# Two loads of keys and queries issued by ScalarE, and two copies moved to VectorE

## The chip, the cores and the metric

The kernel runs on one core of a Trainium2 chip. Times are device microseconds of one execution, from the first to the last work of the core and what lies around it. A core has five engines, each with its own instruction stream in order: TensorE (PE) for matrix products, VectorE (DVE), ScalarE (ACT), GpSimd (POOL) and SyncE (SP), which here only issues transfers between the memory of the chip and the buffers of the core. The engines wait for one another and for transfers by semaphores.

## What is computed

The reference has two parts. The first is gated linear attention over 4 batches, 8 heads, 768 positions and 48 features per head:

```
f = 1 / (1 + exp(-f_logit))
for t in range(S):
    state = f[:, :, t, :, None] * state + k[:, :, t] (outer) v[:, :, t]
    y[:, :, t] = q[:, :, t] @ state
x = y, heads side by side: (4, 768, 384)
```

The second is a gated block with a mixing over positions:

```
h = max(x @ w_in, 0);  u, v = halves of h (512 features each)
v_n = (v - mean(v)) / sqrt(var(v) + 1e-6)
v_s = w_spatial @ v_n (over positions) + b_spatial
out = (u * v_s) @ w_out
```

## The kernel before, in words

The 4 x 768 positions are cut into 24 units of 128 positions, six for each batch. Each unit passes through the attention in chunks, with all eight heads at once, and its result is transposed, split into a high and a low part and used in the products of the second half.

The order of the work isn't found by a planner. It is written out by hand, as a list of words (PLAN, lines 44 to 113), and each word is one step on one unit: `k:0` is step k on unit 0. The program walks through the list and emits each step, so on each engine the instructions stand in the order of the list. A second list (BESIDES, lines 116 to 123) names the steps that are done in the other way that their function knows, for the most part on another engine: `c:2` stands in it, so the clamp of unit 2 is GpSimd's and not VectorE's.

The steps that matter at the start, for unit n:

- **LF** (line 354) loads the logits of the forget gate into the first plane of the input buffer `fkq` (three such buffers, taken in turn by n mod 3, so that unit 3 takes unit 0's). For the first eight units it is a load of 128 x 384 values, 192 KB. **LK** (line 361) loads keys and queries into the second and third plane, 512 KB. **LQ** (line 365) loads values, 192 KB. **LV** (line 297) loads words of a weight, 768 KB. SyncE issues all of them.
- **c** (line 369) clamps the logits, **e** (line 373) takes two activations of them on ScalarE, **z** (line 378) forms running sums on TensorE with a triangular matrix.
- **g** (line 396) and **h** (line 391) take exponentials of the sums on ScalarE. g writes into the first plane of `fkq`.
- **k** (line 401) multiplies the keys by g's result and **q** (line 405) the queries by h's, both on VectorE. k is the last reader of the first plane, so LF of three units later waits for it.
- **X** (line 424) forms the scores of the unit on TensorE, with the queries and, beside them in the same operand, an identity matrix. **m** (line 441) masks them on VectorE, **w** (line 437) copies the part that came from the identity on ScalarE, **YS**, **kv** and **Yq** (lines 477, 449, 486) are further products on TensorE, **r0**, **r1**, **r2** (lines 458, 466, 473) carry the state on.
- **kq** (line 271) puts that identity beside the queries, by two copies from `ident` into buffer i of `q`. It is done once for each of the three buffers, on ScalarE for i = 0, on VectorE for i = 1 (it stands in BESIDES) and on GpSimd for i = 2. **kz** (line 257) clears a part of two accumulators with two memsets on VectorE.

The table of functions of ScalarE is loaded ahead of all this (line 157). In the list the words begin so:

```
LF:0 constants kq:0 LF:2 c:2 kz c:0 e:0 LF:1 c:1 LK:0 e:2 e:1 z:0 g:0 z:2 LK:1 kq:1 k:0 LK:2 h:0 q:0 LQ:0 z:1
D:1,2,512 g:1 k:1 LV:1 X:0 LF:3 ...
```

So SyncE issues LF:0, LF:2, LF:1, LK:0, LK:1, LK:2, LQ:0, LV:1, LF:3 in this order, VectorE does its memsets, c:0, c:1, kq:1, k:0, q:0, k:1, and ScalarE the table, kq:0, e:0, e:2, e:1, g:0, h:0, g:1.

Of the kernel before, what the change touches and what calls it, by code (L numbers as in the profile page):

```python
# [29 lines left out]
P = 128  # L30
# [15 lines left out]
    D:1,2,512 g:1 k:1 LV:1 X:0 LF:3 LQ:1 m:0 h:1 q:1 g:2 k:2 fm:1 LV:0 w:0 YS:0 kv:0 r0:0 X:1 r1:0 c:3 Yq:0 ca:V,1 LF:5
    fm:0 e:3 LK:3 z:3 LF:4 m:1 ct:V,1 r2:0 h:2 w:1 ys:0 YS:1 kv:1 q:2 xt:0 X:2 r0:1 r1:1 c:5 Yq:1 ca:V,0 g:3 xh:0 xl:0
    m:2 k:3 D:2,2,512 r2:1 h:3 q:3 w:2 ys:1 e:5 LQ:2 YS:2 LQ:3 c:4 e:4 ct:V,0 LK:5 X:3 kv:2 w:3 ch:V,0 r0:2 r1:2 m:3
    ch:V,1 xt:1 cl:V,0 z:4 z:5 cl:V,1 xh:1 xl:1 Yq:2 r2:2 YS:3 kv:3 r0:3 fm:2 LF:6 g:4 LK:4 k:4 V:0,0 g:5 h:4 q:4 c:6
    ys:2 xt:2 r1:3 xh:2 xl:2 LU:0 LQ:4 k:5 LK:6 ca:U,0 ct:U,0 e:6 V:0,1 vr:0,1 Yq:3 X:4 w:4 fm:3 ch:U,0 r2:3 h:5 m:4 z:6  # L50
    kq:2 vr:0,0 V:0,2 cl:U,0 ys:3 q:5 YS:4 kv:4 g:6 k:6 r0:4 vr:0,2 nm:0,0 r1:4 X:5 m:5 LF:7 c:7 e:7 z:7 LU:1 ca:U,1
    ct:U,1 xt:3 vc:0,0 fm:5 fm:4 r2:4 h:7 w:5 h:6 q:6 vc:0,2 U:0,0,1 ur:0,0,1 Yq:4 ys:4 LQ:5 YS:5 kv:5 r0:5 LK:7 q:7
    vc:0,1 xh:3 xl:3 g:7 k:7 X:6 LW:2,0 Yq:5 ch:U,1 w:6 xt:4 xh:4 m:6 cl:U,1 LQ:6 xl:4 ys:5 V:0,3 LF:8 c:8 sq:0,0 sq:0,1
    sq:0,2 xt:5 xh:5 X:7 LF:9 na:0,0 r1:5 xl:5 nb:0,0 nc:0,0 w:7 e:8 LQ:7 YS:6 kv:6 r0:6 LF:10 m:7 vh:0,1 vl:0,1 r1:6
    r2:6 z:8 vh:0,0 wh:2,0 vl:0,0 U:0,0,2 V:0,5 YS:7 Yq:6 LW:0,1 c:9 e:9 fm:6 kv:7 U:0,1,3 h:8 q:8 g:8 vr:0,5 U:0,0,3
    ys:6 k:8 X:8 r0:7 r1:7 Yq:7 fm:8 z:9 LQ:9 LW:1,0 LB LQ:8 LF:11 bs:0,5 r2:7 ur:0,0,2 wh:0,1 fm:7 m:8 wl:2,0 wl:0,1
    ur:0,0,3 h:9 q:9 vr:0,3 g:9 k:9 LW:0,0 U:0,1,1 xt:6 vh:0,2 vl:0,2 ur:0,1,3 bs:0,3 w:8 ys:7 V:0,4 vr:0,4 xh:6 wh:1,0
    YS:8 kv:8 r0:8 LQ:10 X:9 w:9 fm:9 LF:12 bs:0,4 r1:8 na:0,1 xl:6 wh:0,0 nb:0,1 wl:1,0 m:9 c:10 e:10 xt:7 xh:7 nc:0,1
    xl:7 r2:8 vn:0,5 vh:0,5 vn:0,4 vh:0,4 V:1,0 Yq:8 YS:9 kv:9 vn:0,3 vh:0,3 vl:0,5 r0:9 wl:0,0 r1:9 vl:0,3 vl:0,4 V:1,1
    vr:1,1 U:0,0,0 S:0,0,2 LO:1 moe ca:O,1 ct:O,1 z:10 vr:1,0 c:11 e:11 sg:0,0,2 r2:9 h:10 g:10 q:10 k:10 ys:8 ch:O,1  # L60
    S:0,0,0 sg:0,0,0 sm:0,0,2 z:11 S:0,0,3 sg:0,0,3 cl:O,1 LQ:11 LW:2,1 wh:2,1 wl:2,1 xt:8 xh:8 xl:8 sh:0,0,2 sl:0,0,2
    X:10 Yq:9 m:10 h:11 q:11 fm:11 bs:1,0 fm:10 g:11 k:11 bs:1,1 ys:9 w:10 c:12 e:12 V:1,2 S:0,0,1 ur:0,0,0 vr:1,2 z:12
    LW:1,1 wh:1,1 wl:1,1 sg:0,0,1 sm:0,0,1 sh:0,0,1 sm:0,0,0 sh:0,0,0 xt:9 xh:9 X:11 YS:10 bs:1,2 sm:0,0,3 w:11 kv:10
    r0:10 m:11 r1:10 r2:10 na:1,0 sl:0,0,0 h:12 g:12 S:0,1,3 sl:0,0,1 q:12 LF:13 LO:0 ca:O,0 k:12 sg:0,1,3 S:0,1,2 Yq:10
    ys:10 ur:0,1,1 xl:9 YS:11 kv:11 X:12 r0:11 Yq:11 c:13 nb:1,0 r1:11 e:13 ct:O,0 ch:O,0 z:13 h:13 g:13 sg:0,1,2
    S:0,1,0 xt:10 fm:13 xh:10 nc:1,0 vn:1,2 vn:1,1 q:13 S:0,1,1 vh:1,1 w:12 LF:15 LQ:12 LF:14 sg:0,1,0 xl:10 sh:0,0,3
    sl:0,0,3 vn:1,0 c:14 vh:1,2 cl:O,0 m:12 vl:1,2 U:0,1,2 ur:0,1,2 V:1,3 ys:11 xt:11 O:0,0,0 sm:0,1,3 vr:1,3 sh:0,1,3
    sl:0,1,3 LQ:13 k:13 YS:12 kv:12 r0:12 X:13 xh:11 xl:11 Yq:12 sg:0,1,1 c:15 V:1,4 U:0,1,0 ys:12 e:15 z:15 e:14 z:14
    bs:1,3 oc:0,0,0 r1:12 r2:12 LF:16 fm:12 m:13 mr1 h:14 q:14 LQ:14 O:0,0,1 ur:0,1,0 sm:0,1,0 oc:0,0,1 w:13 g:14
    O:0,0,2 k:14 c:16 vh:1,0 sm:0,1,1 sh:0,1,1 sh:0,1,0 fm:14 YS:13 kv:13 r0:13 sm:0,1,2 sh:0,1,2 X:14 Yq:13 r1:13  # L70
    vl:1,1 LQ:15 r2:13 sl:0,1,0 vl:1,0 h:15 vr:1,4 V:1,5 sl:0,1,2 vr:1,5 bs:1,5 bs:1,4 na:1,1 sl:0,1,1 nb:1,1 nc:1,1
    vn:1,4 vn:1,5 g:15 U:1,0,1 ur:1,0,1 fm:15 ys:13 oc:0,0,2 od:0,0,1 vn:1,3 U:1,1,3 ur:1,1,3 vh:1,5 m:14 vl:1,5 k:15
    vh:1,3 vl:1,3 vh:1,4 q:15 vl:1,4 LF:17 od:0,0,0 O:0,1,2 O:0,1,0 oc:0,1,2 od:0,1,2 S:1,0,0 sg:1,0,0 YS:14 e:16 w:14
    kv:14 LQ:16 X:15 r0:14 oc:0,1,0 Yq:14 ys:14 r1:14 r2:14 z:16 h:16 q:16 fm:16 w:15 m:15 U:1,0,0 ur:1,0,0 xt:12
    S:1,0,2 S:1,1,3 g:16 k:16 X:16 LF:18 w:16 sm:1,0,0 sg:1,1,3 sm:1,1,3 mr0 c:17 e:17 c:18 YS:15 kv:15 LQ:17 m:16 r0:15
    r1:15 LF:19 z:17 r2:15 h:17 g:17 k:17 sh:1,0,0 O:0,1,1 fm:17 oc:0,1,1 e:18 sl:1,0,0 q:17 S:1,0,1 sg:1,0,1 xt:14
    Yq:15 ys:15 xh:12 xl:12 X:17 LF:20 sg:1,0,2 YS:16 kv:16 r0:16 r1:16 sm:1,0,1 r2:16 S:1,0,3 S:1,1,0 c:19 c:20 Yq:16
    z:18 h:18 fm:18 w:17 q:18 m:17 YS:17 kv:17 g:18 k:18 ys:16 X:18 sg:1,0,3 od:0,0,2 LQ:18 sg:1,1,0 LF:21 r0:17 Yq:17
    xt:13 xh:14 xl:14 od:0,1,0 e:19 z:19 h:19 g:19 U:1,0,3 ur:1,0,3 e:20 V:2,2 vr:2,2 ys:17 w:18 xh:13 U:1,0,2 ur:1,0,2
    V:2,0 vr:2,0 sm:1,0,3 m:18 k:19 q:19 X:19 LF:22 c:21 r1:17 YS:18 kv:18 LQ:20 LQ:19 z:20 sm:1,0,2 xl:13 m:19 sh:1,0,3  # L80
    sh:1,0,1 xt:15 xh:15 w:19 bs:2,0 sh:1,0,2 sl:1,0,2 xl:15 e:21 r0:18 r1:18 sl:1,0,1 r2:18 xt:17 S:1,1,1 xh:17 xl:17
    fm:19 h:20 g:20 k:20 xt:16 xh:16 V:2,1 q:20 Yq:18 ys:18 YS:19 kv:19 r0:19 sg:1,1,1 r1:19 r2:19 z:21 X:20 w:20
    S:1,1,2 LF:23 m:20 h:21 vr:2,1 sl:1,0,3 O:1,0,0 bs:2,1 fm:21 g:21 sh:1,1,3 Yq:19 ys:19 YS:20 kv:20 LQ:22 k:21
    sg:1,1,2 q:21 X:21 bs:2,2 na:2,0 nb:2,0 r0:20 sl:1,1,3 xl:16 nc:2,0 vn:2,0 vn:2,1 c:22 e:22 z:22 V:2,4 O:1,0,2 c:23
    e:23 w:21 r1:20 r2:20 m:21 fm:20 oc:1,0,0 h:22 q:22 oc:1,0,2 vh:2,1 od:0,1,1 LQ:21 U:1,1,2 xt:18 g:22 k:22 Yq:20
    YS:21 kv:21 r0:21 ys:20 X:22 w:22 r1:21 z:23 r2:21 vn:2,2 ur:1,1,2 vr:2,4 h:23 g:23 fm:23 q:23 m:22 U:1,1,0 k:23
    U:1,1,1 xh:18 Yq:21 vh:2,2 ur:1,1,1 ys:21 YS:22 kv:22 r0:22 r1:22 sm:1,1,1 X:23 m:23 ur:1,1,0 fm:22 flag sm:1,1,0
    xt:19 O:1,0,1 sh:1,1,1 sl:1,1,1 w:23 xt:20 xh:19 xl:19 oc:1,0,1 vh:2,0 r2:22 LQ:23 YS:23 od:1,0,0 kv:23 r0:23 Yq:22
    ys:22 sh:1,1,0 check Yq:23 xl:18 bs:2,4 U:2,0,1 ys:23 mst LY:1 V:2,5 V:2,3 sm:1,1,2 sh:1,1,2 LY:2 xh:20 LY:3 ts:1
    ts:3 vl:2,0 sl:1,1,0 vl:2,1 vr:2,5 bs:2,5 sl:1,1,2 V:3,0 U:2,0,0 vr:2,3 bs:2,3 na:2,1 nb:2,1 nc:2,1 vn:2,3 O:1,1,2  # L90
    U:2,0,3 U:2,0,2 O:1,1,1 th:1 ur:2,0,1 vn:2,5 vh:2,5 vl:2,2 ts:2 LY:4 ts:4 od:1,0,2 vn:2,4 xl:20 V:3,2 th:4 vl:2,5
    tl:4 vh:2,4 vl:2,4 tl:1 ur:2,0,3 th:2 vh:2,3 vl:2,3 xs:2,1,1 P:2,0,2 th:3 tl:3 ur:2,0,0 oc:1,1,1 oc:1,1,2 od:1,1,2
    xs:2,1,3 xs:2,1,2 xt:23 xh:23 xl:23 tl:2 mwin ah:2,1,1 P:2,0,1 P:2,1,2 P:2,1,1 p1:2,0 xs:2,0,1 xs:2,0,3 xs:2,0,2
    ah:2,0,2 ur:2,0,2 p1:2,1 xs:2,0,4 ah:2,0,3 V:3,1 xt:22 c1:2,0 ah:2,1,2 al:2,1,2 al:2,0,2 xt:21 P:2,0,6 xs:2,1,4
    ah:2,1,4 P:2,1,6 c1:2,1 al:2,0,3 p2:2,0 V:3,5 P:2,0,7 xh:22 xl:22 xh:21 ah:2,1,3 al:2,1,3 vr:3,2 bs:3,2 vr:3,0
    sm:2,0,1 sh:2,0,1 al:2,1,4 al:2,1,1 p2:2,1 V:3,4 sl:2,0,1 ah:2,0,1 al:2,0,1 sm:2,0,0 P:2,1,5 p3:2,0 xl:21 bs:3,0
    vr:3,1 bs:3,1 na:3,0 nb:3,0 ah:2,0,4 al:2,0,4 load vr:3,4 vr:3,5 V:3,3 vr:3,3 bs:3,3 U:2,1,0 bs:3,5 P:2,0,5 p5:2,0
    bs:3,4 nc:3,0 na:3,1 nb:3,1 nc:3,1 P:2,0,4 P:2,1,7 c4:2,0 sm:2,0,2 vn:3,0 vh:3,0 O:1,1,0 oc:1,1,0 vn:3,1 vn:3,4
    P:2,1,4 P:2,0,3 p5:2,1 U:2,1,2 vn:3,5 od:1,1,0 vh:3,4 vn:3,2 vh:3,1 sh:2,0,0 vl:3,0 vn:3,3 c5:2,1 p3:2,1 vl:3,4
# [905 lines left out]
```

## Time and profile before

| | |
|---|---|
| time, median of 3 runs | 340.78 us (339.2 to 341.7) |
| the profiled execution | 337.91 us, its span 336.2 us |
| granted TensorE clock | 0.999 of full speed |
| TensorE busy | 324.4 us, 96% of the span |
| VectorE busy | 252.4 us, 75% |
| ScalarE busy | 182.7 us, 54% |
| GpSimd busy | 39.7 us, 12% |
| transfers | 38.37 MB, 114 GB/s over the span |

The span runs from the first to the last instruction of the profiled execution; its own time is 1.71 us longer. A share of busy time is a mean over stages that have different limits, so the rows below are read by stage. In a timeline a row is one instruction or several of one kind merged (x3), and the bracket at its end says how long the engine stood idle before it, and what ended that. In the chain of waits each piece is what the next one waited for. Issue of a transfer and its landing are two things: the queue of SyncE is busy only with the issue.

### The profile page before, as it was taken

How to read it: one execution, taken by the hardware profiler on the slowest of the kernel's cores; microseconds unless marked ns; L12 is line 12 of the kernel's file. 1: busy time of each engine (PE TensorE's matmuls, PEld its weight loads, DVE VectorE, ACT ScalarE, POOL GpSimd, SP SyncE). 2: the span in 40 equal slices, each digit the busy share in tenths (PEclk: the TensorE clock that was granted, in tenths of full speed). 3: DMA queues.
4: the chain of work that ended last, by engine and by line, in shares of the span. 5: the costliest groups of instructions: out<-in, count | busy, mean ns of one | idle time of the engine just before them, and what ended most of it. 6: DMA issues, size and time to landing. Idle time of an engine off the chain costs nothing.

```text
span 336.2 us, 10500 instructions
## 1 busy us (share of the span) xinstructions
PE 324.4 (96%) x4558; PEld 303.5 (90%) x4558; DVE 252.4 (75%) x498; ACT 182.7 (54%) x389; POOL 39.7 (12%) x44
## 2 busy tenths in 40 slices
...
GB/s 230 368 225 280 268 176 225 218 173 47 152 89 237 41 89 155 82 62 126 137 120 142 96 73 202 156 0 24 2 0 0 49 0 25 71 0 26 48 34 118
DMA packets 16581, 38.37 MB, mean 114 GB/s; under 512 B 1552, under 2 KB 11792, under 8 KB 16528
## 3 DMA queue, kind: packets, MB, share of 16 engines
...
q8 instruction: 38, 0.62, 0.7%
...
HBM read 32.90 MB, written 4.72 MB: 112 GB/s over the span
## 4 chain that ended last, share of the span: by engine, by line
PE 93%; DMA 3%; DVE 1%; ACT 1%; issue 1%; SPq 0%; DVEq 0%; ACTq 0%
PE mm L664 15%; PE mm L547 13%; PE mm L650 13%; PE mm L803 12%; PE mn L739 8%; PE bp L432 5%; PE mm L739 5%; PE bp L496 4%; PE bp L484 3%; PE mn L803 3%; PE mn L650 3%; PE mm L509 2%; PE bp L456 2%; PE mn L547 2%; DMA fkq<-fkq 2%; DMA fkq<-fn 1%
## 5 line engine op out<-in xcount | busy, mean ns | idle before, releaser
L371 POOL TENSOR_SCALAR fkq<-fkq 112x512 f32<-112x512 f32 (+1 forms) x13 | 22.5, 1729 | 140.2 <-DMA fkq<-fkq 121.8
L789 DVE TENSOR_TENSOR gl<-uT,gh 128x384 fp32r<-128x384 f32 x29 | 16.6, 580 | 19.9 <-ACT gh L785 19.6
L785 ACT CAST gh<-uT 128x384 fp32r<-128x384 f32 x29 | 14.4, 511 | 20.0 <-DVE uT L781 9.8
L392 ACT ACTIVATE F<-fkq 112x512 f32<-112x512 f32 x16 | 10.1, 632 | 26.6 <-DVE fkq L381 14.9
L432 PE MATMUL bp<-q,fkq 48*64 48x112 f32 x768 | 23.6, 260 | 0.1
L403 DVE SCALAR_TENSOR_TENSOR fkq<-fkq 112x512 f32<-112x512 f32 x24 | 16.7, 694 | 5.9 <-ACT fkq L397 4.7
L432 PEld LDWEIGHTS bp<-q,fkq 48*64 48x64 f32 x768 | 19.0, 133 | 2.1 <-issue 1.4
L664 PE MATMUL mm<-w_sph,vnh 128*128 128x384 f32 x96 | 20.1, 345 | 0.0
L381 DVE TENSOR_TENSOR_SCAN fkq<-runs,fkq 112x512 f32<-112x512 bf16 x16 | 19.4, 1217 | 0.5 <-ACT fkq L376 0.4
L664 PE MATMUL mm<-w_spl,vnh 128*128 128x384 f32 x96 | 19.5, 338 | 0.0
L664 PE MATMUL mm<-w_sph,vnl 128*128 128x384 f32 x96 | 19.5, 338 | 0.0
L547 PE MATMUL mm<-w_inh,xTh 128*128 128x512 f32 x63 | 19.2, 412 | 0.0
L650 PE MATMUL mm<-xTh,w_inh 128*128 128x384 f32 x78 | 18.7, 348 | 0.0
L442 DVE TENSOR_TENSOR sc<-bp,mask 128x512 f32<-128x512 f32 x24 | 16.4, 684 | 2.5 <-ACT W L438 2.1
L407 DVE TENSOR_TENSOR q<-fkq,F 112x512 f32<-112x512 f32 x24 | 16.7, 694 | 2.1 <-ACT F L392 2.0
L547 PE MATMUL mm<-w_inl,xTh 128*128 128x512 f32 x63 | 18.1, 396 | 0.0
L547 PE MATMUL mm<-w_inh,xTl 128*128 128x512 f32 x63 | 18.0, 394 | 0.0
L650 PE MATMUL mm<-xTl,w_inh 128*128 128x384 f32 x78 | 17.9, 338 | 0.0
L650 PE MATMUL mm<-xTh,w_inl 128*128 128x384 f32 x78 | 17.9, 337 | 0.0
L484 PEld LDWEIGHTS bp<-val,sc 64*64 64x64 f32 x768 | 13.9, 134 | 4.3 <-issue 1.5
L484 PE MATMUL bp<-val,sc 64*64 64x48 f32 x768 | 16.1, 220 | 1.4 <-DVE sc L442 0.9
L664 PEld LDWEIGHTS mm<-w_spl,vnh 128*128 128x128 f32 x96 | 17.1, 188 | 0.0
...
## 6 DMA issues: line engine op xcount, KB each, us to landing
...
val<-vv SPq DMA_DIRECT2D x24, 192.0 KB, 4.5
out<-osb SPq DMA_DIRECT2D x24, 192.0 KB, 2.4
fkq<-fkq SPq DMA_DIRECT2D x8, 512.0 KB, 5.5
...
fkq<-fn SPq DMA_DIRECT2D x8, 192.0 KB, 4.1
...
```

The lines of the kernel that those rows point to most:

```text
L371: (nc.gpsimd if beside("c", n) else nc.vector).tensor_scalar(f, f, -LOGIT_MOST, None, op0=ALU.max)
L381: return nc.vector.tensor_tensor_scan(f[0:DP], runs, f[0:DP], 0.0, op0=ALU.mult, op1=ALU.add)
L403: nc.vector.scalar_tensor_tensor(k, f, 1.0 / F_LEAST, k, op0=ALU.min, op1=ALU.mult)
L407: nc.vector.tensor_tensor(q_of(n)[:, :, :, 0:C], *(x.rearrange("p (j c t) -> p j c t", c=T // C, t=C) for x in (parts(n)[2], Fs[n % 2])), ...
L432: nc.tensor.matmul(sc[to, e, cs], k[dr, at:at + C], q_of(n)[dr, j, chunk], start=True, stop=True)
L484: nc.tensor.matmul(y[to, e, cs], s[rows, keys[e]], v[rows, hd], start=j == 0, stop=False, skip_group_check=True)
L547: nc.tensor.matmul(acc, xs[:, c, ut * P:(ut + 1) * P], ws[:, c, G:FF], start=i == 0, stop=i == 3 * KX - 1)
L650: nc.tensor.matmul(acc[:, 0:TH], ws[:, kx, cs], xs[:, kx, :], start=i == 0, stop=i == 3 * KX - 1)
L664: nc.tensor.matmul(acc[:, 0:TH], vns.of((b, ks))[va][:, cs], w_sp_s[wb][:, ks, th * TH:(th + 1) * TH], start=i == 0, stop=i == 3 * KS - 1,)
L739: nc.tensor.matmul(mm.of(user)[:, 0:TH], x, y, start=n == ks == 0 and i not in (3, 6, 7), stop=n == ks == 2, skip_group_check=True,)
L789: nc.vector.tensor_tensor(lo, uTs.of((b, th, c)), hi.bitcast(F32), op=ALU.subtract)
L803: nc.tensor.matmul(acc[:, ms], gs.of((b, th, c))[ga][:, ts], w_out_s[wb][:, c, ms], start=c == cs[0] == 0 and ga == wb == 0, stop=c == cs[ ...
```

## The change

LK:0 and LK:2 are issued by ScalarE, and they stand right behind the constants in the list, ahead of LF:2 and LF:1. kq:0 is done by VectorE and stands behind kz, ahead of c:0. Everything else stands in the same order as before. LK:1, and LK of all other units, stay with SyncE. SyncE's order becomes LF:0, LF:2, LF:1, LK:1, LQ:0, LV:1, LF:3.

```diff
 PLAN = """
-    LF:0 constants kq:0 LF:2 c:2 kz c:0 e:0 LF:1 c:1 LK:0 e:2 e:1 z:0 g:0 z:2 LK:1 kq:1 k:0 LK:2 h:0 q:0 LQ:0 z:1
+    LF:0 constants LK:0 LK:2 LF:2 c:2 kz kq:0 c:0 e:0 LF:1 c:1 e:2 e:1 z:0 g:0 z:2 LK:1 kq:1 k:0 h:0 q:0 LQ:0 z:1 D:1,2,512
...
 BESIDES = """
...
-    sm:3,0,1 P:3,1,5 sm:3,0,2 U:3,1,3 P:3,1,3
+    sm:3,0,1 P:3,1,5 sm:3,0,2 U:3,1,3 P:3,1,3 kq:0 LK:0 LK:2
...
     def step_LK(n):
         b, u = divmod(n, NU)
-        nc.sync.dma_start(ins[n % 3][:, 1:3], fkq[b, u, :, 1:3])
+        (nc.scalar if beside("LK", n) else nc.sync).dma_start(ins[n % 3][:, 1:3], fkq[b, u, :, 1:3])
```

The other lines of PLAN hold the same words, broken into lines elsewhere.

## Rows read from the trace of the kernel before

**Rows 1.** The page's chain that ended last, its share of the span by engine.

```profile
PE 93%; DMA 3%; DVE 1%; ACT 1%; issue 1%; SPq 0%; DVEq 0%; ACTq 0%
```

**Rows 2.** Windows: length, busy us of each engine (instructions), granted clock, DMA share, GB/s.

```profile
40.00:240.00 200.00, 200.00 (x3233) 185.87 (x3232) 166.53 (x324) 120.58 (x259) 19.51 (x11) 1.00 0.38 122
```

**Rows 3.** Chain of waits in order of time, to 21 us: start, us, what.

```profile
2.19 5.89 DMA fkq<-fkq
...
8.19 0.70 DVE fkq L403
...
8.91 4.73 DMA fkq<-fn
...
13.66 0.62 DVE fkq L371
...
20.55 0.68 PE bp L484 x32
```

**Rows 4.** Timeline of ScalarE, to 8 us: start, us, engine, line, operation, idle before.

```profile
0.80 1.28 ACT L157 ACT_TABLE_LOAD   x1 [0.80 <-PEq L998]
2.10 1.03 ACT L276 COPY q<-ident 48x384 f32<-48x384 f32 x2
3.77 0.52 ACT L375 ACTIVATE fkq<-fkq 128x384 f32<-128x384 f32 x1 [0.65 <-DVE fkq L371]
...
6.40 0.52 ACT L375 ACTIVATE fkq<-fkq 128x384 f32<-128x384 f32 x1
...
7.38 0.58 ACT L397 ACTIVATE fkq<-mm 112x512 f32<-112x512 f32 x1
```

**Rows 5.** Windows of the start, columns as in rows 2.

```profile
1.40:1.80 0.40, 0.00 (x0) 0.00 (x0) 0.25 (x4) 0.40 (x1) 0.33 (x2) 1.00 0.00 0
1.80:3.40 1.60, 0.00 (x0) 0.00 (x0) 0.65 (x3) 1.31 (x3) 0.50 (x3) 1.00 0.90 269
3.40:4.20 0.80, 0.00 (x0) 0.00 (x0) 0.34 (x1) 0.42 (x1) 0.22 (x1) 1.00 0.67 109
...
5.00:16.00 11.00, 8.72 (x204) 7.57 (x206) 7.81 (x15) 7.63 (x15) 1.02 (x4) 1.00 1.02 366
```

**Rows 6.** Timeline of VectorE and GpSimd, 1 to 14 us.

```profile
1.68 0.79 DVE L259 MEMSET bp<- 32x384 f32 x2
...
3.38 0.36 DVE L371 TENSOR_SCALAR fkq<-fkq 128x384 f32<-128x384 f32 x1 [0.92 <-DMA fkq<-fn]
3.98 1.17 POOL L371 TENSOR_SCALAR fkq<-fkq 128x384 f32<-128x384 f32 x1 [1.63 <-DMA fkq<-fn]
6.00 0.36 DVE L371 TENSOR_SCALAR fkq<-fkq 128x384 f32<-128x384 f32 x1 [2.26 <-DMA fkq<-fn]
6.28 0.72 DVE L276 COPY q<-ident 48x384 f32<-48x384 f32 x2
...
9.96 0.69 DVE L403 SCALAR_TENSOR_TENSOR fkq<-fkq 112x512 f32<-112x512 f32 x1 [0.47 <-ACT fkq L397]
...
10.80 0.69 DVE L442 TENSOR_TENSOR sc<-bp,mask 128x512 f32<-128x512 f32 x1 [0.15 <-PE bp L432]
...
13.66 0.61 DVE L371 TENSOR_SCALAR fkq<-fkq 128x384 f32<-128x384 f32 x1 [0.21 <-DMA fkq<-fn]
```

**Rows 7.** Timeline of SyncE's queue, 0 to 4 us.

```profile
0.81 1.34 SPq L357 DMA_DIRECT2D fkq<-fn  x3
2.19 1.38 SPq L363 DMA_DIRECT2D fkq<-fkq  x3
```

**Rows 8.** DMA issues near 0.81, 1.72, 2.65, 3.14: KB each, us to landing.

```profile
fkq<-fn SPq DMA_DIRECT2D x1, 192.0 KB, 2.6
...
fkq<-fn SPq DMA_DIRECT2D x1, 192.0 KB, 4.3
...
fkq<-fkq SPq DMA_DIRECT2D x1, 512.0 KB, 6.7
...
fkq<-fkq SPq DMA_DIRECT2D x1, 512.0 KB, 7.5
```

More of the change, by code (lines that the diff above doesn't have):

```diff
@@ L44 @@
 PLAN = """
-    LF:0 constants kq:0 LF:2 c:2 kz c:0 e:0 LF:1 c:1 LK:0 e:2 e:1 z:0 g:0 z:2 LK:1 kq:1 k:0 LK:2 h:0 q:0 LQ:0 z:1
[L46 to L99, printed above, removed]
@@ L100 @@
-    c4:2,1 c3:2,0 c5:2,0 sm:2,0,3 vh:3,5 vl:3,5 vh:3,3 U:2,1,1 vl:3,3 xs:3,0,1 sl:2,0,0 ur:2,1,2 sm:2,1,2 U:3,0,0
-    P:2,1,3 ur:3,0,0 P:3,1,2 c3:2,1 U:2,1,3 ah:3,0,1 sh:2,0,2 vh:3,2 sh:2,0,3 od:1,0,1 xs:3,1,1 xs:3,1,3 vl:3,2 vl:3,1
-    P:3,1,1 sl:2,0,2 sl:2,0,3 O:2,0,0 O:2,0,1 oc:2,0,1 ur:2,1,1 sm:2,1,1 r1:23 sh:2,1,1 sl:2,1,1 U:3,0,3 oc:2,0,0
-    od:2,0,0 od:1,1,1 ah:3,1,3 ur:2,1,0 ur:2,1,3 sm:2,1,3 O:2,0,2 oc:2,0,2 od:2,0,2 P:3,0,1 U:3,0,1 P:3,1,4 xs:3,1,2
-    p1:3,0 xs:3,0,3 xs:3,0,2 p1:3,1 od:2,0,1 al:3,1,3 sm:2,1,0 sh:2,1,0 P:3,0,2 c1:3,1 xs:3,1,4 ah:3,1,2 al:3,1,2
@@ L105 @@
-    P:3,1,6 p2:3,1 U:3,0,2 al:3,0,1 P:3,0,5 xs:3,0,4 sl:2,1,0 ah:3,0,3 ur:3,0,1 al:3,0,3 c1:3,0 sm:3,0,0 U:3,1,0 P:3,1,7
-    ah:3,0,2 al:3,0,2 P:3,0,6 p3:3,1 c4:3,1 sh:2,1,2 sl:2,1,2 ah:3,1,1 al:3,1,1 U:3,1,1 ah:3,1,4 p2:3,0 sh:2,1,3
-    sl:2,1,3 P:3,0,7 P:3,0,4 p5:3,0 sm:3,0,1 sh:3,0,1 sl:3,0,1 ur:3,0,2 ur:3,0,3 p3:3,0 c5:3,0 sm:3,0,3 sh:3,0,3
-    ah:3,0,4 P:3,1,5 O:2,1,0 oc:2,1,0 od:2,1,0 O:2,1,2 oc:2,1,2 od:2,1,2 U:3,1,2 ur:3,1,2 p5:3,1 O:2,1,1 oc:2,1,1
-    od:2,1,1 sh:3,0,0 al:3,0,4 c4:3,0 sm:3,0,2 sh:3,0,2 sl:3,0,3 sm:3,1,2 sh:3,1,2 ur:3,1,0 sl:3,0,2 c5:3,1 sl:3,1,2
@@ L110 @@
-    sl:3,0,0 al:3,1,4 U:3,1,3 ur:3,1,3 sm:3,1,3 ur:3,1,1 sh:3,1,3 P:3,0,3 c3:3,0 sm:3,1,0 O:3,0,2 P:3,1,3 O:3,0,1
-    O:3,0,0 sh:3,1,0 sl:3,1,3 c3:3,1 sm:3,1,1 sh:3,1,1 sl:3,1,1 oc:3,0,0 od:3,0,0 oc:3,0,1 od:3,0,1 oc:3,0,2 od:3,0,2
-    sl:3,1,0 O:3,1,2 oc:3,1,2 O:3,1,0 oc:3,1,0 O:3,1,1 oc:3,1,1 end od:3,1,2 od:3,1,0 od:3,1,1
+    LF:0 constants LK:0 LK:2 LF:2 c:2 kz kq:0 c:0 e:0 LF:1 c:1 e:2 e:1 z:0 g:0 z:2 LK:1 kq:1 k:0 h:0 q:0 LQ:0 z:1 D:1,2,512
+    g:1 k:1 LV:1 X:0 LF:3 LQ:1 m:0 h:1 q:1 g:2 k:2 fm:1 LV:0 w:0 YS:0 kv:0 r0:0 X:1 r1:0 c:3 Yq:0 ca:V,1 LF:5 fm:0 e:3 LK:3
```

63 lines of the change are left out of this document (added).

## The prediction

> **What bounds the kernel now.** I read the chain of waits first. TensorE holds 93% of it [rows 1], and the windows say where: from 40 to 240 us it is busy for all of the 200 us [rows 2], and the chain enters TensorE at 20.55 us and hardly leaves it again [rows 3]. From there on the end follows TensorE's start one for one: what the change is worth is by how much that entry moves. Everything that is edited stands in the first five microseconds, so I read the chain in order of time up to there. It comes out of a load of SyncE that is issued at 2.19 and lands 5.89 us later, at 8.08 [rows 3]. That is LK:0, the keys and queries of unit 0. VectorE's k:0 waits for it and starts at 8.19; it frees the first plane of the buffer, so SyncE issues LF:3 at 8.91, which lands at 13.63 and lets VectorE start c:3 at 13.66. VectorE then works almost without a stop until TensorE takes the chain over.
>
> Two more views give the room beside this chain. ScalarE's timeline [rows 4]: e:0, e:2, e:1, g:0 in this order. g:0 starts at 7.38 straight behind e:1, and ends at 7.96. So k:0, which needs g:0 and LK:0, waits only about 0.2 us for the load (8.19 against 7.96 plus the 0.03 or so that an issue takes). The DMA windows [rows 5]: 269 GB/s up to 3.4 us, 109 from 3.4 to 4.2, and 366 from 5 to 16 us with the share of busy time at 1.02. The transfer engines are full from 5 us on, and have a hole of about 0.8 us before.
>
> **The change, part by part.** All terms are against the profiled execution, 337.91 us, of which 336.2 are the span and 1.71 lie around it. It stands 2.87 under the median of 340.78, so I carry differences over, not times.
>
> *The copies of kq:0.* On ScalarE two copies (1.03 together, from 2.10) go away [rows 4]; on VectorE two of the same shape come, 0.72 together as the pair of kq:1 shows [rows 6]. They stand behind the two memsets of kz, which end at 2.47, and ahead of c:0, which starts at 3.38 when LF:0 lands: 2.47 + 0.72 = 3.19 fits, with 0.19 to spare. Cost nothing; without that cover (LF:0 landing earlier) at most 0.72 less the wait that is left. No consumer is near: X:0 reads them, and it stands behind k:0 and q:0, after 8.19.
>
> *The two issues on ScalarE.* Three issues on SyncE take 1.38 [rows 7], 0.46 each with the gap. On ScalarE no issue is shown. If each costs the same, LK:0 and LK:2 take 0.92. Behind the table load, which ends at 2.08 [rows 4], that is over at 3.00, ahead of e:0 at 3.77: nothing. For the lower bound nothing is gained, as e:0 waits for c:0 anyway; for the upper one, issues of three times this length would push e:0 by 1.1. I take zero: an issue costs about that much in every row of rows 7.
>
> *What SyncE no longer issues.* Its order becomes LF:0, LF:2, LF:1, LK:1, LQ:0, LV:1. LK:1 is issued at 2.19 instead of 2.65, LQ:0 near 2.65 instead of 3.61, LV:1 about 0.95 earlier. k:1 waits for g:1, not for LK:1 (2.65 + 6.7 = 9.35 [rows 8], k:1 starts at 9.96 [rows 6]), so the earlier LK:1 is worth nothing by itself. LK:2 lands at 3.14 + 7.5 = 10.64 [rows 8], and its first reader on VectorE stands behind m:0 and q:1, both later (m:0 starts at 10.80 [rows 6]): nothing to gain there either.
>
> *When LK:0 lands.* The trace has no transfer on a second queue, so this is bounded. Early end: it is there before g:0 ends. Then k:0 starts at 7.99 instead of 8.19, 0.20 gained; q:0, X:0 and m:0 follow, but m:0 can't start ahead of k:1's end (9.96 + 0.69 = 10.65, against 10.80), so 0.15 is left; and LF:3, issued 0.2 earlier into engines that have used their hole, can take away what is left of VectorE's wait before c:3, 0.21 [rows 6]. The sum is 0.36 at most. Late end: LK:0 shares the engines with LK:1 and lands only when LK:1 does now, at 9.35: k:0 1.2 later, of which the wait before c:3 gives 0.21 back, so +1.0. Now it lands at 8.08 behind three small loads, alone in front. I take 8.1 again: about 0.1 us earlier at the issue (2.08 against 2.19) and bytes in the hole (0.8 us at 366 less 109 GB/s are 0.2 MB, 0.55 us of later traffic) on one side, LK:1's bytes between its own on the other. Term: 0.
>
> *What the loads of forget logits lose.* LF:0, LF:2 and LF:1 are ahead of e:0, e:2, e:1, and these ahead of g:0. LF:1 is issued at 1.72 and lands 4.3 later, near 6.0 [rows 8]; c:1 starts at 6.00 and e:1 at 6.40 [rows 4, 6], when e:2 (two activations of 0.52 behind c:2, which ends at 3.98 + 1.17 = 5.15) has ended near 6.3. There is no slack left: each microsecond that LF:1 is later is one at g:0. With LK:0 issued behind the table load its first bytes come, as LF:0's did (issued at 0.81, first bytes after 1.8 us [rows 5]), about 1 us later, near 3.1, when LF:0 has nearly landed; what can be hit is the rest of LF:1. Bounds 0 and +1.6 (next part); I take 0, because in the stretch where LF:1 finishes the engines carry the least [rows 5].
>
> Sum: 0. Forecast: **no change that can be measured, 340.8 us**. Its own range is -0.4 to +0.4.
>
> A rule of the Trainium skill speaks against any gain: DMA: Bandwidth & Descriptors, section "Issuing engines are not separate DMA queues", says that loads issued by ScalarE and SyncE run on the same 16 engines and interleave, so that a second issuer saves only issue time. By it the late end above is the likely one and the sum would be that of the second rival; no run here shows two queues at once yet.
>
> **The rivals.** *First, slower: the forget logits come late.* If ScalarE's sequencer sends LK:0 while the table load still runs, it is issued at about 0.8, level with LF:0, and LK:2 right behind. Then each of the three small loads (197 KB) carries as many bytes of the large ones with it. LF:0 comes 197 KB late, 0.7 at 269 GB/s; LF:2 393 KB late, 1.46, so at 5.4 instead of 3.95, just ahead of c:2's start at 3.98; c:2 on GpSimd takes 1.17 [rows 6], e:2 ends near 7.7; LF:1 590 KB late, 1.6 at 366 GB/s, lands near 7.55, c:1 and e:1 follow and g:0 starts near 8.93 instead of 7.38. k:0 then starts at 9.55, +1.36; LF:3's load of 4.7 us had about 2.2 of queue in it (LF:0 took 2.6 [rows 8]), so it is in time, and the wait before c:3 gives 0.21 back: +1.1, 341.9. It decides as soon as c:1 starts later than 6.1. For it: no slack before g:0. Against: the copies of kq:0 started 0.02 behind the table load's end, as if ScalarE took things in turn, but a DMA issue isn't such an operation. Chance 0.2.
>
> *Second, slower: LK:0 shares with LK:1.* Issue behind the table load, but the engines serve both queues evenly, and LK:0 lands between 8.1 and 9.35; the hole's 0.55 speaks for less than the late end. Taking 9.0, k:0 is 0.9 late: +0.7, 341.5. Chance 0.2.
>
> *Third, faster: the hole is filled.* LK:0 lands before 7.96 and LF:3 in time: -0.35, 340.4. For it: 109 GB/s where 366 are possible. Against: VectorE gets only the two short waits of the early end. Chance 0.2.
>
> The forecast has 0.35; the 0.05 left are for things that I can't price, such as an issue on ScalarE that is several times as long, or a fixed cost of a second queue outside the span.
>
> **How the numbers follow.** All cases lie between -0.4 and +1.1 us. The three runs of the kernel before spread from 1.6 under their median to 0.9 over it, and this enters the range: 340.8 - 0.4 - 1.6 = 338.8, 340.8 + 1.1 + 0.9 = 342.8; I end it at 342.6, since both upper ends together are less likely. About 1%, 3.4 us, is what a measurement of this kernel can tell from no change. A gain of 3.4 is nine times the largest that the waits allow: 0.04, for what the spread or something unseen may do. A loss of 3.4 is three times the largest price: 0.05. Within 1%: 0.91.
>
> **What will show it.** In the changed profile: issues of LK:0 and LK:2 on ScalarE's queue, with their start against the table load's end at 2.08 (first rival or not); c:0 still at 3.4 with kq:0's copies in front of it; c:1 at 6.0 and g:0 at 7.4 (LFs not late); k:0's start against g:0's end (LK:0's landing); GB/s between 3.4 and 4.2 us (hole filled or not); c:3's wait; and TensorE's entry into its unbroken run at 20.55 give or take 0.4, with the same work behind it. The prediction is wrong if that entry moves by more than 1.5 us, or if it doesn't and the span changes all the same.

## The result, and the profile after

The changed kernel takes 341.78 us (median of 20 runs, 339.88 to 343.45), the kernel before 340.14 (20 runs, 337.91 to 341.70). The ratio is 1.0064, with a 95% interval from 1.0048 to 1.0080: about 2.2 us slower (1.6 to 2.7); the two medians alone lie 1.6 apart. Ratios leave out executions more than 1.5% above the fastest of their kernel, in which the granted clock was 0.985 of full speed or less. The result is inside the range and within 1%, but it isn't the likeliest case of the prediction: it is the first rival's mechanism, at twice its price.

From the page of the profile after, its span, TensorE's busy time, and the second queue (packets, MB, share of 16 engines):

```profile
span 339.8 us, 10500 instructions
...
PE 326.3 (96%) x4558; PEld 304.3 (90%) x4558; DVE 253.0 (74%) x500; ACT 181.5 (53%) x387; POOL 40.9 (12%) x44
...
q10 hardware_dynamic: 288, 1.05, 0.8%
```

It is 10500 instructions and 38.37 MB, as before; 1.05 MB of these now pass through a second queue, q10. The timeline of the start answers to [rows 4, 6, 7]:

```profile
0.80 1.28 ACT L154 ACT_TABLE_LOAD   x1 [0.80 <-PEq L995]
...
0.83 0.88 ACTq L360 DMA_DIRECT2D fkq<-fkq  x2
...
2.19 0.83 SPq L360 DMA_DIRECT2D fkq<-fkq  x1
2.38 0.71 DVE L273 COPY q<-ident 48x384 f32<-48x384 f32 x2
...
4.71 0.36 DVE L368 TENSOR_SCALAR fkq<-fkq 128x384 f32<-128x384 f32 x1 [1.62 <-DMA fkq<-fn]
...
6.33 1.95 PE L383 MATMUL mm<-tri,fkq 128*64 128x128 f32 x16 [6.33 <-ACT fkq L373]
6.63 1.17 POOL L368 TENSOR_SCALAR fkq<-fkq 128x384 f32<-128x384 f32 x1 [3.82 <-DMA fkq<-fn]
7.52 0.49 DVE L368 TENSOR_SCALAR fkq<-fkq 128x384 f32<-128x384 f32 x1 [2.45 <-DMA fkq<-fn]
7.84 0.52 ACT L372 ACTIVATE fkq<-fkq 128x384 f32<-128x384 f32 x1 [1.65 <-POOL fkq L368]
...
9.79 0.58 ACT L394 ACTIVATE fkq<-mm 112x512 f32<-112x512 f32 x1
...
10.40 0.69 DVE L400 SCALAR_TENSOR_TENSOR fkq<-fkq 112x512 f32<-112x512 f32 x1 [1.75 <-ACT fkq L394]
...
12.76 0.60 ACT L394 ACTIVATE fkq<-mm 112x512 f32<-112x512 f32 x1 [1.91 <-PE mm L383]
```

Line by line: ScalarE's queue issues the two loads at 0.83, while the table load of 0.80 to 2.08 still runs. VectorE's copies of kq:0 fit in front of c:0, as expected. But c:0 starts at 4.71 instead of 3.38, c:2 on GpSimd at 6.63 instead of 3.98, c:1 at 7.52 instead of 6.00, e:2 at 7.84, and g:0 at 9.79 instead of 7.38. k:0 no longer waits for its load (its bracket names ScalarE) and starts at 10.40 instead of 8.19 all the same.

The issues near 0.83, 0.81, 1.3, 1.25 and 1.72 (KB each, us to landing), which answer to [rows 8]:

```profile
fkq<-fkq ACTq DMA_DIRECT2D x1, 512.0 KB, 4.3
fkq<-fn SPq DMA_DIRECT2D x1, 192.0 KB, 3.9
...
fkq<-fkq ACTq DMA_DIRECT2D x1, 512.0 KB, 6.0
fkq<-fn SPq DMA_DIRECT2D x1, 192.0 KB, 5.2
...
fkq<-fn SPq DMA_DIRECT2D x1, 192.0 KB, 5.8
```

The logits land 3.9, 5.2 and 5.8 us after their issue, at 4.7, 6.5 and 7.5; before it was 2.6 and 4.3 for the first and the last. LK:0 lands at 5.1, ahead of LF:2 and LF:1, where nobody wants it yet. The windows (columns as in rows 2) show that the hole of [rows 5] is filled, 371 GB/s where 109 were:

```profile
1.80:3.40 1.60, 0.00 (x0) 0.00 (x0) 1.25 (x4) 0.29 (x1) 0.96 (x3) 1.00 0.89 225
3.40:4.20 0.80, 0.00 (x0) 0.00 (x0) 0.00 (x0) 0.00 (x0) 0.00 (x0) 1.00 0.94 371
4.20:5.00 0.80, 0.00 (x0) 0.00 (x0) 0.29 (x1) 0.00 (x0) 0.00 (x0) 1.00 1.07 399
```

The chain of waits (start, us, what) now comes out of LF:2, passes through GpSimd's clamp and e:2 and reaches TensorE's sums of units 2 and 1, behind which g:1, k:1 and X:0 stand. It no longer passes through k:0 and LF:3, the path that the prediction had read [rows 3]:

```profile
1.25 5.21 DMA fkq<-fn
...
6.63 1.18 POOL fkq L368
...
8.96 3.68 PE mm L383 x31
```

TensorE's entry into its unbroken run is at 24.08 instead of 20.55 [rows 3]. That is 3.5 us, where the prediction had set 1.5 as the sign that it is wrong. The work behind it has the same length (339.8 - 24.08 = 315.7, before 336.2 - 20.55 = 315.7):

```profile
24.08 0.68 PE L481 MATMUL bp<-val,sc 64*64 64x48 f32 x32 [0.51 <-ACT W L435]
```

This pair of profiles gives 3.5 us, more than the ratio. The first profile of the kernel before is its shortest execution of the 20 (337.91); a second profile of this kernel stands below.

### The profile page after: what moved, and what is told of

Read it like the earlier page. It is cut to its first block, busy times and chain, and to the rows that moved or that the text cites. A ratio compares the mean times of both kernels' runs of the same rounds, so it can differ in the third digit from the quotient of the medians.

```text
span 339.8 us, 10500 instructions
## 1 busy us (share of the span) xinstructions
PE 326.3 (96%) x4558; PEld 304.3 (90%) x4558; DVE 253.0 (74%) x500; ACT 181.5 (53%) x387; POOL 40.9 (12%) x44
## 2 busy tenths in 40 slices
DMA packets 16581, 38.37 MB, mean 113 GB/s; under 512 B 1552, under 2 KB 11792, under 8 KB 16528
## 3 DMA queue, kind: packets, MB, share of 16 engines
q10 hardware_dynamic: 288, 1.05, 0.8%
## 4 chain that ended last, share of the span: by engine, by line
PE 93%; DVE 2%; DMA 2%; ACT 1%; issue 1%; POOL 0%; SPq 0%; DVEq 0%; ACTq 0%; POOLq 0%
PE mm L661 15%; PE mm L544 13%; PE mm L647 12%; PE mm L800 12%; PE mn L736 8%; PE bp L429 6%; PE mm L736 5%; PE bp L493 3%; PE bp L481 3%; PE mn L800 3%; PE mn L647 3%; PE mm L506 2%; PE bp L453 2%; PE mm L383 2%; PE mn L544 2%; DMA fkq<-fn 2%
## 5 line engine op out<-in xcount | busy, mean ns | idle before, releaser
L383 PE MATMUL mm<-tri,fkq 128*64 128x128 f32 (+1 forms) x128 | 10.8, 332 | 7.8 <-ACT fkq L373 7.8
L372 ACT ACTIVATE fkq<-fkq 112x512 f32<-112x512 f32 (+1 forms) x24 | 14.3, 594 | 6.0 <-DVE fkq L368 4.2
```

What stands on the lines that cost most here:

```text
L383: nc.tensor.matmul(z[lo:hi, j * T:(j + 1) * T], f[:, at:at + hi - lo], tri, start=True, stop=True)
```

## The experiments

Starts in us in the profile of each run; the entry is the first product of unit 2's YS on TensorE. Ratios are to runs of the kernel before on the same chip, from 12 runs of each variant (one_queue 6, warm_after 7). In the profiles marked * the granted clock fell to 0.50 of full speed, the 1.2 GHz level, for some us at the start (warm_after from 23 to 29 us, unit1_first from 20 to 26, unit1_first_z2_late from 17 to 20), so their entries and spans don't compare with the others.

| kernel | c:0 | c:2 | c:1 | g:0 | entry | span | ratio (95%) |
|---|---|---|---|---|---|---|---|
| before | 3.38 | 3.98 | 6.00 | 7.38 | 20.55 | 336.2 | |
| before_again | 3.13 | 3.80 | 5.52 | 6.95 | 20.90 | 337.1 | |
| changed | 4.71 | 6.63 | 7.52 | 9.79 | 24.08 | 339.8 | 1.0064 (1.0048 to 1.0080) |
| kq_alone | 3.17 | 3.82 | 5.27 | 6.97 | 20.86 | 336.9 | 1.0014 (0.9988 to 1.0040) |
| loads_alone | 4.57 | 6.42 | 7.24 | 9.57 | 22.46 | 338.2 | 1.0084 (1.0054 to 1.0114) |
| loads_behind_kq | 3.14 | 3.90 | 7.96 | 9.34 | 21.63 | 339.1 | 1.0051 (1.0028 to 1.0074) |
| one_queue | 3.26 | 7.75 | 8.12 | 11.09 | 24.90 | 341.1 | 1.0168 (1.0141 to 1.0195) |
| half_early | 4.29 | 5.45 | 6.48 | 8.61 | 22.21 | 338.4 | 1.0046 (1.0019 to 1.0073) |
| logits_two_queues | 3.74 | 4.08 | 4.46 | 7.42 | 21.51 | 338.7 | 1.0016 (0.9993 to 1.0040) |
| warm_after * | 4.71 | 6.51 | 7.39 | 9.67 | 23.77 | 345.4 | 1.0096 (1.0060 to 1.0132) |
| warm_after_again | 4.76 | 6.56 | 7.42 | 9.71 | 22.16 | 341.2 | |
| warm_before | 3.16 | 3.86 | 5.43 | 7.01 | 21.91 | 338.3 | 1.0039 (1.0008 to 1.0071) |
| unit1_first * | 3.28 | 5.82 | 3.90 | 7.20 | 23.77 | 340.0 | 0.9989 (0.9964 to 1.0013) |
| unit1_first_z2_late * | 3.17 | 5.06 | 3.91 | 7.07 | 21.89 | 337.7 | 1.0044 (1.0014 to 1.0074) |

**The two parts of the change, one at a time.** First the copies alone, with LK:0 and LK:2 where they were:

```diff
-    LF:0 constants kq:0 LF:2 c:2 kz c:0 ...
+    LF:0 constants LF:2 c:2 kz kq:0 c:0 ...      (kq:0 in BESIDES)
```

> Only kq:0 moves to VectorE; all loads as before. Theory (the loss is the two large loads in front of LF:2 and LF:1): no loss; c:0 starts at 3.4, g:0 at 7.4, TensorE's entry at about 20.6, ratio 1.000 (0.998 to 1.002). Rival (the copies on VectorE cost, since in the changed kernel GpSimd's mask copy beside them took 0.70 and not 0.24): c:0 later than 3.6 and a ratio from 1.003 to 1.006.

Measured: 1.0014, the interval holds 1; c:0 at 3.17 and g:0 at 6.97. GpSimd's mask copy took 0.70 here too, and nobody waits for it. Then the loads alone:

```diff
-    LF:0 constants kq:0 LF:2 ...
+    LF:0 constants LK:0 LK:2 kq:0 LF:2 ...       (LK:0, LK:2 in BESIDES)
```

> Only LK:0 and LK:2 move to ScalarE, in front of kq:0, which stays with ScalarE. Theory (early large loads): as the whole change: issues at 0.83, c:0 at 4.7, LF:2 landing near 6.5, g:0 near 9.8, ratio 1.005 to 1.008. Rival (the copies): c:0 at 3.4 and a ratio below 1.003.

Timeline of this kernel:

```profile
4.57 0.36 DVE L368 TENSOR_SCALAR fkq<-fkq 128x384 f32<-128x384 f32 x1 [2.10 <-DMA fkq<-fn]
...
6.42 1.17 POOL L368 TENSOR_SCALAR fkq<-fkq 128x384 f32<-128x384 f32 x1 [4.08 <-DMA fkq<-fn]
...
8.75 2.92 PE L383 MATMUL mm<-tri,fkq 128*64 128x128 f32 x32 [0.62 <-ACT fkq L373]
...
9.57 0.58 ACT L394 ACTIVATE fkq<-mm 112x512 f32<-112x512 f32 x1
```

1.0084, and the same late starts as in the changed kernel. The loss is the loads': the copies alone have 1 in their interval.

**When they are issued.**

```diff
-    LF:0 constants kq:0 LF:2 ...
+    LF:0 constants kq:0 LK:0 LK:2 LF:2 ...       (LK:0, LK:2 in BESIDES)
```

> kq:0 stays with ScalarE and stands in front of LK:0 and LK:2, so that these two are issued by ScalarE only once the identity matrix is there, near 2.1, as the forecast had assumed. Theory (it is the moment of issue that costs): c:0 at 3.4, LF:2 landed by 4.5, g:0 by 8.0, k:0 between 8.0 and 9.0, ratio 0.999 to 1.003. Rival (a second queue takes its share whenever it is issued): LF:1 lands after 7 all the same, g:0 after 8.5, ratio above 1.004.

Timeline of this kernel:

```profile
1.92 0.38 ACTq L360 DMA_DIRECT2D fkq<-fkq  x1
...
3.90 1.17 POOL L368 TENSOR_SCALAR fkq<-fkq 128x384 f32<-128x384 f32 x1 [1.55 <-DMA fkq<-fn]
...
7.96 0.36 DVE L368 TENSOR_SCALAR fkq<-fkq 128x384 f32<-128x384 f32 x1 [4.46 <-DMA fkq<-fn]
...
9.34 0.58 ACT L394 ACTIVATE fkq<-mm 112x512 f32<-112x512 f32 x1
```

The theory, that the moment of issue decides, fell, and the rival held: with the issue at 1.92, LF:0 and LF:2 are in time (c:0 3.14, c:2 3.90), but LF:1, issued at 1.72 and so 0.2 ahead, lands only for c:1 at 7.96. Since g:0 stands behind e:1, it starts at 9.34, nearly as late as in the changed kernel. It isn't the early moment that costs: a large load on the second queue delays the last of the logits also when it is issued behind them. The transfers up to the landing of LF:1 (queue, packets, MB, share) tell how much. First the kernel before, from 1.80 to 5.98 us:

```profile
q1 hardware_dynamic: 552, 1.06, 90.0%
```

Then this kernel, from 1.80 to 7.92:

```profile
q1 hardware_dynamic: 553, 1.03, 53.1%
q10 hardware_dynamic: 212, 0.80, 39.5%
```

SyncE's queue q1 moved as much as before, so it isn't what SyncE now issues earlier that delays LF:1. The 0.80 MB of q10 come on top, about 2 us at the 390 GB/s that the window of 7 to 8 us shows (an estimate), and LF:1 lands 2.0 later.

**Which queue.** The list of the changed kernel, but SyncE issues all of it, so LK:0 and LK:2 stand between LF:0 and LF:2 in one queue.

```diff
-    sm:3,0,1 ... P:3,1,3 kq:0 LK:0 LK:2
+    sm:3,0,1 ... P:3,1,3 kq:0
```

> The list in the order of the changed kernel and kq:0 on VectorE, but LK:0 and LK:2 issued by SyncE: LF:0, LK:0, LK:2, LF:2, LF:1, LK:1 in one queue. Theory (1 MB in front of LF:2 and LF:1, whichever queue it is in): c:0 at 3.4 since LF:0 is alone in front, LF:2 lands near 7, LF:1 near 7.5, g:0 between 9 and 10, ratio 1.004 to 1.008. Rival (the loss comes from two queues taking turns): LF:2 and LF:1 no later than 6, g:0 by 8, ratio below 1.003.

Timeline of this kernel:

```profile
3.26 0.36 DVE L368 TENSOR_SCALAR fkq<-fkq 128x384 f32<-128x384 f32 x1 [0.17 <-DMA fkq<-fn]
...
7.75 1.36 POOL L368 TENSOR_SCALAR fkq<-fkq 128x384 f32<-128x384 f32 x1 [4.93 <-DMA fkq<-fn]
8.12 0.36 DVE L368 TENSOR_SCALAR fkq<-fkq 128x384 f32<-128x384 f32 x1 [4.50 <-DMA fkq<-fn]
...
11.09 0.58 ACT L394 ACTIVATE fkq<-mm 112x512 f32<-112x512 f32 x1
```

The theory's cause held, its size didn't: without any second queue the loss is largest, 1.0168 where at most 1.008 was expected. LF:0 is untouched, LF:2 lands behind all of the 1 MB, g:0 starts at 11.09 (9 to 10 expected). Taking turns isn't the cost; it even softens it. The counterpart takes the second queue for a load of logits and leaves the keys and queries behind them:

```diff
-    LF:0 constants kq:0 LF:2 c:2 ...
+    LF:0 LF:2 constants kq:0 c:2 ...             (LF:2 in BESIDES, step_LF as step_LK in the change)
```

> The kernel before, in which ScalarE issues LF:2 (the 192 KB of logits of unit 2) while SyncE issues LF:0; all keys and queries stay behind the logits on SyncE. Theory (what counts is which bytes are in front of the logits, not the second queue): LF:0 at most 0.5 us later, LF:1 lands 0.4 us earlier or as before, g:0 between 7.0 and 7.6, ratio 0.997 to 1.001. Rival (a second queue itself costs): c:0 after 4.2, g:0 after 8.2, ratio above 1.003.

Timeline of this kernel:

```profile
3.74 0.36 DVE L371 TENSOR_SCALAR fkq<-fkq 128x384 f32<-128x384 f32 x1 [1.27 <-DMA fkq<-fn]
...
4.46 0.36 DVE L371 TENSOR_SCALAR fkq<-fkq 128x384 f32<-128x384 f32 x1 [0.36 <-DMA fkq<-fn]
...
7.42 0.58 ACT L397 ACTIVATE fkq<-mm 112x512 f32<-112x512 f32 x1
```

c:0 is 0.4 late, c:1 1.5 early, g:0 as before; 1.0016 with 1 in the interval. A second queue by itself costs nothing that can be measured here.

**How many bytes.** Only LK:0 is issued early by ScalarE; LK:2 follows LK:1 on SyncE.

```diff
-    LF:0 constants LK:0 LK:2 LF:2 ... k:0 h:0 ...
+    LF:0 constants LK:0 LF:2 ... k:0 LK:2 h:0 ...    (kq:0 and LK:0 in BESIDES)
```

> The changed kernel with only LK:0 issued early by ScalarE; LK:2 is issued by SyncE behind LK:1, as before. Theory (bytes in front of the logits of units 2 and 1): half the bytes, so LF:2 lands near 5.2 instead of 6.5, LF:1 near 6.9, g:0 starts near 8.8 (7.4 before, 9.8 changed), ratio to before between 1.002 and 1.005. Rival (any use of a second queue so early costs the same, whatever the size): g:0 at 9.5 or later, ratio from 1.006.

Timeline of this kernel:

```profile
5.45 1.17 POOL L368 TENSOR_SCALAR fkq<-fkq 128x384 f32<-128x384 f32 x1 [2.63 <-DMA fkq<-fn]
...
8.61 0.58 ACT L394 ACTIVATE fkq<-mm 112x512 f32<-112x512 f32 x1
```

Half the bytes, 5.45 for c:2 and 8.61 for g:0, between before and the changed kernel, as priced; 1.0046 is about 70% of the loss, though the intervals are wide.

**Does TensorE's pace add to it?** In the first profile of the kernel before, the 48 sums of units 0, 2 and 1 took 4.22 us; in the changed kernel 16 took 1.95 and 32 took 3.68, 122 and 115 ns each. Products of constants in front of z:0 let TensorE work from 1.66 on.

```diff
-    ... e:2 e:1 z:0 g:0 z:2 ...
+    ... e:2 e:1 D:0,11,512 z:0 g:0 z:2 ...           (D:0,7,512 in warm_before)
```

> The changed kernel with eleven more products of constants in front of z:0 on TensorE (nobody reads their result), so that it works from about 1.6 us on. Theory (a part of the loss is that the 32 sums of units 2 and 1 ran at 115 ns each, the slower pace, up to 12.6 us): these run at about 57 ns, g:1 starts near 11 instead of 12.76, TensorE's entry is 1 to 1.8 us earlier than 24.1, ratio to before 1.001 to 1.004. Rival (pace is off the path, late logits alone set the time): ratio 1.006 to 1.008 as changed.

> The kernel before with seven such products in front of z:0. Theory (pace matters where it is late): g:1 starts at 8.5 instead of 9.33, but k:1 then waits for q:0 on VectorE, so 0.3 to 0.9 us are gained at the entry, ratio 0.997 to 1.000. Rival (z:0 is held up by the added products or pace is off the path): 1.000 or more.

Both came out against the theory: 1.0096 and 1.0039. In warm_before the loss goes with the granted clock of the executions: five with a clock of 0.994 or more took 338.5 to 340.2, like the kernel before on that chip (median 339.5), and the seven with 0.980 to 0.992 took 340.0 to 343.8. In warm_after it doesn't: the six executions in its ratio had 0.995 or more and took 341.5 to 343.8. Against the 1.0064 of the changed kernel the intervals overlap, so the eleven products gave nothing back, and whether they cost more isn't shown.

The profile of warm_after is of its longest execution, 347.18 us. It shows a granted clock of 0.66 in this window (the column behind the five engines), a mean of 1.00 and of 0.50, the 1.2 GHz level; TensorE had then worked since 1.66 us:

```profile
20.00:30.00 10.00, 8.46 (x183) 7.00 (x177) 8.18 (x15) 6.88 (x14) 2.44 (x4) 0.66 0.74 237
```

A second profile of the same kernel is without that:

> The changed kernel with eleven early products once more, for a profile without the low granted clock at 20 to 30 us. Theory (what the earlier pace wins by 18 us is kept): entry near 22.5 and a span near 338. Rival (it is lost again later, to a lower granted clock or to a load): entry at 23.5 or later, or a lower granted clock, and a span of 340 or more.

Timeline, and TensorE's waits from 24 to 300 us (us in total, times, longest), of the second profile:

```profile
1.66 4.88 PE L265 MATMUL mm<-runs 112*128 112x512 bf16 x11 [1.66 <-DVE runs L215]
...
8.89 2.05 PE L383 MATMUL mm<-tri,fkq 128*64 128x128 f32 x32 [0.96 <-ACT fkq L373]
...
11.06 0.60 ACT L394 ACTIVATE fkq<-mm 112x512 f32<-112x512 f32 x1 [0.29 <-PE mm L383]
...
22.16 0.68 PE L481 MATMUL bp<-val,sc 64*64 64x48 f32 x32
```

```profile
PE mm L544 <- DVE y L686: 2.4, 1, 2.4
```

The pace is as the theory wants: 32 sums in 2.05 us, 64 ns each, g:1 at 11.06 instead of 12.76, the entry at 22.16 instead of 24.08. But 3.3 us are lost later, 2.4 of them in one wait for VectorE at line 686, at 210 to 220 us, which neither the kernel before nor the changed one shows. The rival held. Why the wait is there isn't shown, nor whether other executions have it; but none of the six in the ratio comes near the 339.7 us that go with a span of 338. Now a second profile of the kernel before:

> The kernel before once more, for a second profile: the first one is of its shortest execution of 20. Theory (the moment at which TensorE's pace doubles and the landing of loads differ between executions): a span of 336.5 to 338.5, with the 48 sums of the first three units taking up to 5.3 us where the first profile had 4.22, c:0 at 3.2 to 3.5 and TensorE's entry at 20.6 to 22. Rival: the same as the first profile within 0.3 us everywhere, so that the loss in the profile of the changed kernel (3.6 us) is what it costs.

Timeline of this kernel, and last one piece of its chain of waits (start, us, what):

```profile
4.75 5.36 PE L386 MATMUL mm<-tri,fkq 128*64 128x128 f32 x48 [4.75 <-ACT fkq L376]
...
6.95 0.58 ACT L397 ACTIVATE fkq<-mm 112x512 f32<-112x512 f32 x1
...
20.90 0.68 PE L484 MATMUL bp<-val,sc 64*64 64x48 f32 x32 [0.51 <-ACT W L438]
```

```profile
4.75 5.38 PE mm L386 x48
```

Here the 48 sums took 5.36 us, 112 ns each, the pace of the changed kernel, and the entry is at 20.90 all the same. The slow pace belongs to both kernels; in the first profile it ended early, at about 8 us. The chain of waits is another one here too: it comes out of LF:0, c:0 and e:0 and runs through these 48 sums, and not through LK:0, k:0 and LF:3 as in [rows 3]. The path that the prediction had read is that of one short execution.

Set against this second profile, the last of the changed kernel's 48 sums ends 2.5 us later (12.64 against 10.11). Its next products, still at the slow pace, add 0.65, and the entry is 3.2 later. In loads_alone the logits are as late (g:0 9.57 against 9.79), but the pace rises earlier: 32 sums take 2.92 where the changed kernel has 3.68, and the entry is 1.6 earlier. So up to 1.6 of the 3.2 between the profiles hang on the moment at which TensorE's pace rises. Over many executions this isn't shown to be a part of the loss: loads_alone has the longer ratio of the two, 1.0084, and the profile shown is of nearly its shortest execution (339.89; the shortest took 339.83).

**A better order?** If the last of 48 slow sums holds up g:1, units 1 and 2 should change places (c:1 then stands in BESIDES instead of c:2), and z:2 could wait. The second variant also moves z:2 behind X:0, w:0 ahead of g:2 and k:2 behind r1:0.

```diff
-    LF:0 constants kq:0 LF:2 c:2 kz c:0 e:0 LF:1 c:1 LK:0 e:2 e:1 z:0 g:0 z:2 ... LQ:0 z:1
+    LF:0 constants kq:0 LF:1 c:1 kz c:0 e:0 LF:2 c:2 LK:0 e:1 e:2 z:0 g:0 z:1 ... LQ:0 z:2
```

> The kernel before with units 1 and 2 changing places at the start: LF:1 in front of LF:2, c:1 on GpSimd and c:2 on VectorE, e:1 and z:1 in front of e:2 and z:2. Theory (g:1 and k:1 wait for the last of the 48 sums at TensorE's slow pace): g:1 starts 0.8 to 1.7 us earlier; X:0 still stands behind all 48 sums, so the gain at the entry is at most 0.5, ratio 0.997 to 1.000. Rival (VectorE and the loads set the time): 1.000 or more.

> As unit1_first, and z:2 stands behind X:0 on TensorE, w:0 in front of g:2 on ScalarE, k:2 behind r1:0 on VectorE, so that the scores of unit 0 wait for 32 sums and not for 48. Theory: X:0 starts at 9.5 to 9.7 whatever the pace (9.7 to 11.2 seen), 0.5 to 1 us gained in the executions with the slow pace, ratio 0.996 to 0.999. Rival (z:2's sums then delay YS:0 and h:2 by as much): 1.000 or more.

The first step of both theories came true: g:1 started at 8.59 in unit1_first (9.33 and 10.22 in the two profiles of the kernel before), and X:0 at 9.51 in unit1_first_z2_late. The time didn't follow: 0.9989, with 1 in the interval, and 1.0044, no gain from the first that can be measured and a loss from the second. Four of the twelve executions of the second had a granted clock of 0.985 and took 341.9 to 342.9, which is a part of its loss. None of these versions beats the kernel before.

## Why the prediction was right and wrong

- **The size**: 340.8 was forecast with a range to 342.6, and "within 1%" was given 0.91. The ratio of 1.0064 is within it, and that is owed to the width of the range. The likeliest case, zero, was wrong, and so was its own range of -0.4 to +0.4; both slower rivals together had 0.4. By the sign that the prediction set itself, an entry that moves by more than 1.5 us, it was wrong: the entry moved by 3.5, and by 3.2 against the second profile.
- **The step that failed** is "What the loads of forget logits lose: I take 0". I took it because I thought of LK:0 as issued behind the table load, near 2.1, and of LF:1 as nearly through. The first is wrong: the issue is at 0.83, beside the table load. The second is wrong by itself: loads_behind_kq has the issue at 1.92 and LF:1 lands 2 us late. The reason given, that the engines carry the least where LF:1 finishes, is a misreading of [rows 5]: the hole is from 3.4 to 4.2, and LF:1 lands at 6.0, where the row from 5 us on shows 366 GB/s and a share of 1.02. The slack that I had read correctly, none ahead of g:0, made these microseconds count.
- **The first rival** had the mechanism (issue at 0.8, logits late, g:0 late, TensorE's entry late). Its terms against the measured ones: c:0 4.1, measured 4.71; LF:2 5.4, measured 6.46; LF:1 7.55, measured 7.5; g:0 8.93, measured 9.79; k:0 +1.36, measured +2.21; in all +1.1, measured +2.2. The mis-sized term is LF:2. I let each small load carry as many bytes of the large ones with it, 0.4 MB in all until LF:0 has landed. But by then (1.80 to 4.66 us) the two queues had moved 0.83 MB:

```profile
q10 hardware_dynamic: 147, 0.54, 54.4%
q1 hardware_dynamic: 206, 0.29, 37.9%
```

The second queue had nearly two thirds of the bytes, and LK:0 was nearly through (5.1). So LF:2 came 2.5 us late, and c:2, which takes GpSimd 1.17, then set when e:2, e:1 and g:0 could run; the rival had c:1 there. The path was another one too: the rival went on through k:0 and c:3, while the profile went on through the sums of units 2 and 1.

- **The second rival**, LK:0 late because of LK:1, didn't happen: LK:0 landed at 5.1. It was also where I had put the rule of the Trainium skill (DMA: Bandwidth & Descriptors, "Issuing engines are not separate DMA queues"), that loads issued by several engines run on the same 16 engines and interleave. The trace agrees with the rule: the bytes of both queues passed side by side, and in loads_behind_kq LF:1 was late by what the second queue's bytes take. I had only asked which load the rule would hit behind LK:0, and not which ones ahead of it.
- **The third rival** was right in its first step, the hole is filled (371 GB/s), and this was worth nothing: what fills it are bytes that no engine waits for yet.
- **The copies of kq:0** cost nothing, as worked out: 2.38 + 0.71 = 3.09, ahead of c:0 at 3.17 in kq_alone, ratio 1.0014.
- **One for one from the entry on** holds to 0.7 us in eight profiles: span less entry is 315.7 (before, changed, loads_alone) to 316.4 (kq_alone, before_again, half_early, one_queue, warm_before). It is 317.2 in logits_two_queues, 317.5 in loads_behind_kq and 319.0 in warm_after_again, where TensorE had waits later on. Between the profiles of the two kernels the entry differs by 3.2 to 3.5 us, between loads_alone and before_again by 1.6; the ratio's 2.2 lies between.
